# A bias load cut into five and moved behind the dense weights, to shift the final store in the round of DMA semaphores

## Chip, cores, metric

One core of one Trainium2 chip. The metric is the device time of one execution in microseconds (us). A run also has a span: the time from the first to the last instruction that the profile records on the core.

## The reference, cut to what matters

```python
def reference(A_x, A_k_cache, A_v_cache, A_wq, A_wo, B_x, B_w1, B_b1, B_w2):
    xn = _layernorm(A_x, axis=-1)                  # x: (2, 1, 448)
    # A: one decode step of attention over the last 4096 of 32768 cached rows,
    #    16 query heads on 8 key/value heads of width 256, then wo
    # B: h = xn @ w1 + b1 (1792 wide), act = h * tanh(softplus(h)), act @ w2
    return A_x + A(xn, k_cache, v_cache, wq, wo) + B(xn, w1, b1, w2)
```

The caches make up nearly all of the data: 8 heads x 2 sequences x 4096 rows x 256 x 2 bytes, for K and again for V, 67 MB of the 77.7 MB that are read.

## The kernel before

Every transfer is issued by SyncE, but for x and b1, which ScalarE issues. The framework hands each transfer one of eight DMA semaphores in turn. A transfer that gets a semaphore for the second time has to wait until the earlier one with it has landed.

```python
    x_bf = consts.tile([Bsz, D], BF16)
    nc.scalar.dma_start(out=x_bf[:, :], in_=A_x.flatten_outer_dims())
    b1_sb = consts.tile([NX, HF], BF16)                       # 2 x 896
    nc.scalar.dma_start(out=b1_sb[:, :], in_=B_b1.rearrange("(x f) -> x f", x=NX))
    ...
    for lo, hi in ((0, SC), (SC, NS)):                        # wq in two loads
        nc.sync.dma_start(out=wq_sb[:, lo:hi, :], in_=wq_in[:, lo:hi, :])
    ...
    nc.scalar.activation(out=rstd[:], in_=mv[:, 1:2], func=ACT.Sqrt, bias=eps_t[:], scale=1.0)
    ...
    def load_dense():
        ...
        nc.sync.dma_start(out=dense["w1"], in_=...)
        nc.sync.dma_start(out=dense["w2"], in_=...)

    def dense_in():
        for c in range(NF):
            for s in range(NS):
                nc.tensor.matmul(hT_ps[:, c, ...], lhsT=w1_v[:, s, c, :], rhs=xs[:, s, ...], ...)
            nc.tensor.matmul(hT_ps[:, c, ...], lhsT=b1_v[:, c, :], rhs=half[:], ...)   # adds b1
    ...
    load_k(0)
    load_dense()
    project()                    # q; ScalarE casts half of it
    build_q(0); build_q(1); turn(0)
    for i in range(Hkv + 1):     # per key/value head: load_k(i + 1), load_v(i), load_wo(i), ...
        ...
    res = consts.tile([Bsz, D], BF16)
    for n in range(NO):
        copy = nc.vector.tensor_copy if n // 2 == 0 else nc.scalar.copy
        copy(out=res[:, n * DO : (n + 1) * DO], in_=part(n))
    nc.sync.dma_start(out=out.flatten_outer_dims(), in_=res[:])      # the store
    issue_in_order(tc)           # each engine keeps the order of the text
```

The softmax here doesn't subtract the row's maximum and nothing guards it: scores larger than these inputs give would overflow.

## Time and profile before

| | before |
|---|---|
| time, median of 3 runs | 189.75 us (189.72 to 190.41) |
| profiled run: time, span | 189.68 us, 187.84 us |
| last load lands (last piece of wo) | 184.54 us |
| store issued, landed | 185.59, 186.74 us |
| store issued to end of span | 2.25 us |

The times inside a run are counted from the span's start. The SyncE timeline of the start (start, length, line, what is issued):

```profile
1.65 0.61 SPq L373 DMA_DIRECT2D k<-in_A_k_cache_dram  x1
2.30 0.58 SPq L306 DMA_DIRECT2D v<-in_B_w_dram  x1
2.93 0.44 SPq L313 DMA_DIRECT2D v<-in_B_w_dram  x1
3.41 0.55 SPq L373 DMA_DIRECT2D k<-in_A_k_cache_dram  x1
```

k0, the two dense weights and k1 are all issued within 4 us, long before they land.

### The profile page before, as it was taken

The numbers are of one execution on the slowest core, as the hardware profiler recorded it, in microseconds if no ns is written. First come the engines' busy times: TensorE is split into PE (matmuls) and PEld (weight loads), VectorE is DVE, ScalarE is ACT, GpSimd is POOL, SyncE is SP. The second block draws the span as 40 slices with busy tenths as digits, with TensorE's granted clock in tenths as the row PEclk, the third lists the DMA queues.
The fourth block names the chain that finished last, engine by engine and source line by source line (L and its number), as shares of the span: only waits on it lengthen the run. The fifth ranks groups of instructions, "written<-read, shape, count | busy, mean of one in ns | idle before, by whom it ended". The sixth has DMA issues, their size and how long they took to land.

```text
span 187.8 us, 2412 instructions
## 1 busy us (share of the span) xinstructions
PE 141.0 (75%) x938; PEld 65.0 (35%) x938; DVE 108.6 (58%) x150; ACT 45.3 (24%) x148; POOL 16.3 (9%) x74
## 2 busy tenths in 40 slices
PE   0397098904989989956896769955995779999682
PEld 0132033801334334422342324321441324444581
DVE  6703597049671994079804991099506993995201
ACT  3003115200152244024222224033302332244001
POOL 7000600300003001100030003000110000000000
PEclk9999759955899999999999999999999999999955
DMA  6999899999999999999999999999999999999990
GB/s 224 415 479 447 373 432 457 422 447 447 433 433 426 419 415 437 433 433 400 472 445 426 419 433 433 433 433 409 443 443 440 397 423 433 457 443 391 422 378 31
DMA packets 5030, 77.81 MB, mean 414 GB/s; under 512 B 534, under 2 KB 1052, under 8 KB 2332
## 3 DMA queue, kind: packets, MB, share of 16 engines
q1 hardware_dynamic: 5012, 77.66, 96.9%
q8 instruction: 7, 0.11, 0.2%
q14 instruction: 3, 0.02, 0.0%
q10 hardware_dynamic: 8, 0.01, 0.0%
HBM read 77.67 MB, written 0.00 MB: 413 GB/s over the span
## 4 chain that ended last, share of the span: by engine, by line
DMA 66%; DVE 20%; PE 8%; SPq 2%; ACT 1%; issue 1%; ACTq 0%; DVEq 0%
DMA k<-in_A_k_cache_dram 57%; DVE kt L404 16%; DMA wo<-in_A_wo_dram 9%; PE sc L416 4%; PE o L484 4%; DVE pT L442 3%; SPq L373 2%; ACT p L430 1%; PE psE L217 0%; SPq L114 0%; DVE sums L451 0%; SPq L398 0%; DVE oTm L544 0%; DVE recm L476 0%; PE psA L234 0%
## 5 line engine op out<-in xcount | busy, mean ns | idle before, releaser
L404 DVE STREAM_TRANSPOSE kt<-k 128x2048 f32<-128x2048 f32 x32 | 73.3, 2296 | 51.1 <-DMA k<-in_A_k_cache_dram 51.1
L416 PE MATMUL sc<-kt,qdiag 128*128 128x512 bf16 x256 | 62.1, 387 | 18.8 <-DVE kt L404 18.1
L430 ACT ACTIVATE p<-sc,off 128x256 bf16<-128x256 f32 x64 | 33.0, 542 | 68.4 <-PE sc L416 67.8
L484 PE MATMUL o<-v,pT 128*8 128x512 bf16 x192 | 42.5, 379 | 0.0
L416 PEld LDWEIGHTS <-qdiag 128*128 128x128 bf16 x256 | 22.9, 97 | 54.4 <-issue 16.5
L484 PEld LDWEIGHTS <-pT 128*8 128x8 bf16 x192 | 17.2, 92 | 22.4
L442 DVE STREAM_TRANSPOSE pT<-p 128x512 bf16<-128x512 bf16 x32 | 21.8, 682 | 4.7 <-ACT p L430 4.7
L286 POOL COPY qdiag<-qt 32x16 bf16<-32x16 bf16 x64 | 12.9, 247 | 120.2 <-PE sc L416 103.0
L493 ACT COPY o_sb<-o 8x512 f32<-8x512 f32 x12 | 6.3, 572 | 36.3 <-PE o L484 36.3
L430 ACT ACTIVATION_READ_ACCUMULATOR p<-sc,off 128x1 f32 x64 | 11.6, 182 | 0.0
L217 PE MATMUL psE<-wo,oTm 128*2 128x448 bf16 x24 | 5.5, 351 | 7.2 <-DVE oTm L544 7.2
L266 PE MATMUL q_ps<-v,xq 128*128 128x512 bf16 x28 | 8.7, 487 | 2.1 <-DVE xq L257 2.1
L217 PE MATMUL psE<-v,act_bf 128*2 128x448 bf16 x14 | 4.4, 493 | 7.0 <-DVE act_bf L354 7.0
L563 PE MATMUL q<-pT,v 128*128 128x4 bf16 x256 | 7.8, 169 | 2.5 <-DMA v<-in_A_v_cache_dram 2.3
L563 PEld LDWEIGHTS <-v 128*128 128x128 bf16 x256 | 7.5, 101 | 3.3 <-DMA v<-in_A_v_cache_dram 3.3
L276 DVE CAST q_sb<-q_ps 128x512 bf16<-128x512 f32 x2 | 1.3, 686 | 8.2 <-PE q_ps L266 8.2
L266 PEld LDWEIGHTS <-xq 128*128 128x128 bf16 x28 | 3.3, 121 | 7.5 <-issue 3.3
L217 PEld LDWEIGHTS <-oTm 128*2 128x2 bf16 x24 | 1.5, 82 | 11.3 <-DVE oTm L544 9.7
L217 PEld LDWEIGHTS <-act_bf 128*2 128x2 bf16 x14 | 1.4, 108 | 9.7 <-DVE act_bf L354 7.1
L190 PE MATMUL xnT_ps<-ident,xn_bf 2*128 2x2 bf16 x7 | 0.5, 166 | 5.7 <-DVE xn_bf L138 5.7
L523 PEld LDWEIGHTS q<-ident_f,o_sb 8*128 8x128 f32 x48 | 3.4, 136 | 2.5 <-issue 2.5
L276 ACT CAST q_sb<-q_ps 128x512 bf16<-128x512 f32 x2 | 1.1, 588 | 12.5 <-PE q_ps L266 12.5
(60 smaller groups left out, 49.5 us busy)
## 6 DMA issues: line engine op xcount, KB each, us to landing
k<-in_A_k_cache_dram SPq DMA_DIRECT2D x7, 4096.0 KB, 27.6
v<-in_A_v_cache_dram SPq DMA_DIRECT2D x7, 4096.0 KB, 29.6
k<-in_A_k_cache_dram SPq DMA_DIRECT2D x2, 2048.0 KB, 24.6
v<-in_B_w_dram SPq DMA_DIRECT2D x2, 1568.0 KB, 24.5
wo<-in_A_wo_dram SPq DMA_DIRECT2D x7, 448.0 KB, 30.2
v<-in_A_wq_dram SPq DMA_DIRECT2D x1, 2048.0 KB, 7.4
v<-in_A_v_cache_dram SPq DMA_DIRECT2D x1, 2048.0 KB, 15.2
v<-in_A_wq_dram SPq DMA_DIRECT2D x1, 1536.0 KB
```

The lines of the kernel that those rows point to most:

```text
L217: nc.tensor.matmul(psE[:], lhsT=lhsT, rhs=w, start=start, stop=stop, skip_group_check=True)
L266: nc.tensor.matmul(ps[u][:], lhsT=xq[:, s, :, :].rearrange("p j k -> p (j k)"), rhs=wq_sb[:, s, u * N5 : (u + 1) * N5], start=(s == 0), st ...
L286: nc.gpsimd.tensor_copy(out=tv[rows, :, e, j * Q : (j + 1) * Q : HS].rearrange("p n (b h) -> p n b h", b=Bsz), in_=qv[rows, :, h0 : h0 + r ...
L373: nc.sync.dma_start(out=t[:, cols], in_=src[:, :, cols])
L404: nc.vector.transpose(out=kt[:].bitcast(FP32), in_=k[:, half * TH * Dh : (half + 1) * TH * Dh].bitcast(FP32),)
L416: nc.tensor.matmul(psc[:], lhsT=qdiag[i % NW][:, n * NE + e, :], rhs=ktv[:, n, e, :, :], start=(n == 0 and e == 0), stop=(n == NB - 1 and ...
L430: nc.scalar.activation(out=pv[:, b, :, :], in_=sv[:, b, :, :], func=ACT.Exp, scale=scale, bias=off[:, b : b + 1], accum_out=state["rs", i] ...
L442: nc.vector.transpose(out=pT[:], in_=p_t.pop(s)[:])
L484: nc.tensor.matmul(po[:], lhsT=pT_t[i * NH + piece][:, uh * NP * Q : (uh + 1) * NP * Q : HS], rhs=v[:, u * NP : (u + 1) * NP, :].rearrange ...
L493: nc.scalar.copy(out=o_sb[:, u, :, :, :], in_=po[:, u * Dh : (u + 1) * Dh] .rearrange("r (m j) -> r j m", j=NJ) .unsqueeze(2) .to_broadcas ...
L523: nc.tensor.transpose(pqv[:, j, u, :], o_sb[:, u, j, :, :].rearrange("r h m -> r (h m)"), ident_f[0:NR, 0:NR],)
L563: nc.tensor.matmul(po[:, c, :], lhsT=vv[:, t, c, :], rhs=pTv[:, th, 0:Q:HS], start=(t == 0 and c == 0), stop=(t == T - 1), skip_group_chec ...
```

## The change

The intent: four more transfers, so that the store becomes the eighth of its round and its semaphore is the last one that the program waits for at its end. b1 was chosen to be cut up, because it is small and needed late.

```diff
     b1_sb = consts.tile([NX, HF], BF16)
-    nc.scalar.dma_start(out=b1_sb[:, :], in_=B_b1.rearrange("(x f) -> x f", x=NX))
@@ load_dense, behind w1 and w2
+        b1_in = B_b1.rearrange("(x f) -> x f", x=NX)
+        for u in range(NB1):                                  # NB1 = 5
+            cols = slice(u * HF // NB1, (u + 1) * HF // NB1)
+            nc.scalar.dma_start(out=b1_sb[:, cols], in_=b1_in[:, cols])
```

More of the change, by code (lines that the diff above doesn't have):

```diff
@@ L299 @@
     )
+    NB1 = 5
     act_bf = consts.tile([P, NF, NX, Bsz], BF16)
```

## The prediction

> **What bounds the kernel now.** I read the page first, then the DMA queue's own waits, the chain in order of time near the end, and at last the single records behind the store.
>
> ```profile
> PE 141.0 (75%) x938; PEld 65.0 (35%) x938; DVE 108.6 (58%) x150; ACT 45.3 (24%) x148; POOL 16.3 (9%) x74
> ...
> DMA  6999899999999999999999999999999999999990
> ...
> q1 hardware_dynamic: 5012, 77.66, 96.9%
> ...
> q10 hardware_dynamic: 8, 0.01, 0.0%
> ```
>
> No engine is busy throughout, but the row of the 16 DMA engines is at 8 or 9 tenths from the second slice to the last but one, and SyncE's queue alone (q1) fills 96.9% of them. ScalarE's queue (q10) holds eight packets: those of x and of the bias b1. So the body of the kernel is a full queue of loads, 77.66 MB, and only three things can move the time: the queue running dry, more work for the DMA engines, or what lies before the first byte and after the last. The chain of waits near the end (start, length, what) shows where the last byte lands:
>
> ```profile
> 163.29 0.02 issue
> 163.31 0.54 SPq L373
> ...
> 167.20 17.34 DMA wo<-in_A_wo_dram
> 184.54 0.04 issue
> 184.58 0.46 PE psA L234 x8
> 185.04 0.23 ACT res L639
> 185.28 0.27 ACTq L667
> ```
>
> The last piece of wo is issued at 167.2 and lands at 184.54, having stood 17 us in the queue. After that come the last matmuls, the four casts of the result, and the store. The span is 187.8, so 3.3 us lie behind the last load. In these the trace shows (lines of the SyncE timeline, then the instructions of the kernel's end between 186.7 and 187.15 us: durations in ns, first and last start):
>
> ```profile
> 185.59 0.33 SPq L640 DMA_DIRECT2D out_dram<-res  x1
> ```
> ```profile
> L667 SPq EVENT_SEMAPHORE  x5: 27/28/28, 186.8 to 187.0; - x5
> L667 SPq DRAIN  x2: 7/10/13, 187.1 to 187.1; - x2
> ```
>
> The store is issued at 185.59; its semaphore has its last increment at 186.743. Then SyncE runs five semaphore instructions, which start at 186.759, 186.823, 186.884, 186.949 and 187.010, and a drain at 187.075: 63 ns from one to the next, though each lasts only 28. Each of the five waits for two semaphores. By their numbers in the records: 103 and 102, 107 and 101, 108 and 100, 109 and 104, 110 and 105; the drain waits for 99. The eight DMA semaphores are 100, 101, 102, 103, 107, 108, 109, 110; 104, 105 and 99 are VectorE's, ScalarE's and GpSimd's. The store carries 103, the fourth of the eight, and it stands in the **first** of the five instructions, so the other four are walked through after it has landed.
>
> **What the Trainium skill says.** "Perfetto Trace Analysis", Identifying Dependency Chains: an instruction that has more to wait for gets EventSemaphore instructions in front of it. The trace agrees, with the five above. "Advanced Engine Details and Errata", Network/Comms: a sequencer's read of a semaphore takes 50 to 100 ns; the trace's 61 to 65 ns from one of the five to the next lie inside that. "DMA: Bandwidth & Descriptors", Why a DMA increments its semaphore by 16 and not by 1: a transfer that uses k engines has 16 - k posted at once by the sequencer and the rest as each engine's data lands. The trace agrees: b1, two partitions, has an update at 1.72 us and two single ones at 6.64 and 6.78. So each small transfer touches two DMA engines only. The same page, Specifications: below 512 B the engine does a read-modify-write. The rows of the new transfers have 358 or 360 B; no run here has such packets of data yet.
>
> **The change part by part.**
>
> 1. It removes one load of b1 from ScalarE's start (0.24 us of issue at 1.31 us). What follows there is a table load (1.58 to 2.87) and then the square root, which waits for VectorE until 4.31. The table load may begin 0.27 us earlier and then waits longer. Worth 0.
>
> 2. It adds five loads of b1 on ScalarE behind the square root. One issue costs 0.24 us (b1 before) to 0.55 us (x), so 1.2 to 2.8 us. ScalarE has nothing to do between 4.6 us and the first cast of q at 17.07 (12.5 us idle in the page's groups, waiting for PE). This is hidden, provided that none of the five waits beyond 17 us; see the rivals. The first matmul that reads b1 is at 33.77 us, and it already waits for w1 first. PE has to wait for five semaphores in place of one there, some two more semaphore instructions of 51 ns, on an engine that after these matmuls stands still for 7.0 us until VectorE has act_bf. Worth 0.
>
> 3. It moves the round. In the kernel before a load takes the semaphore of the one eight places ahead of it and waits for that one to have landed. Before: x, wq (first), b1, wq (second), k0, w1, w2, k1, then v0, wo0, k2 and so on. After: five b1 pieces stand between w2 and k1 (or about there), so k1 waits for k0, v0 for w1, wo0 for w2, and k2, v1, wo1, k3, v2 for pieces of b1. From wo2 on each waits for the same load as before, because the distance of eight doesn't change. Landings by the semaphore events: k0 21.46, w1 25.23, w2 29.00, k1 40.0 us. So k1 would be issued at 21.5 and no longer at 3.4, and it would find w1 and w2 still queued, 29.00 - 21.46 = 7.5 us of work. v0 then goes at 25.2 (before 17.5) with k1 queued, wo0 at 29.0. k2 goes at 31.5 in both, when VectorE has freed its buffer. The queue holds at least 7 us at each of these, so no byte lands later. Worth 0.
>
> 4. It moves the store. The program has 36 transfers: 9 of k, 11 of v, 9 of wo, 2 of wq, 2 dense weights, x, b1, the store. 36 = 4 x 8 + 4: the store is the fourth of its round. With four more it is number 40 = 5 x 8, the eighth. If the list at the end keeps its order, the eighth semaphore stands in the fifth of the five instructions. The four ahead wait for things long done and pass while the store is under way: it takes 186.743 - 185.917 = 0.83 us after its issue, and four of them need 4 x 63 = 0.25 us. So the end comes **0.25 us** sooner.
>
> 5. It adds packets. b1 before: on each of two DMA engines one packet of 74 ns and one of 9 ns for the semaphore, 83 ns. x, 896 B, takes 39 to 49 ns; from 74 and 44 my estimate for 358 B is 26 ns. Five of these with five times 9 ns are 175 ns, so some 0.09 us more on two of 16 engines; if the short rows cost double, 0.2 us. That counts only if one of the two is the last to finish. The last wo piece lands on its engines between 182.60 and 184.54 us, and 5 of the 16 are within 0.21 us of the last: a chance of about a half that one of the two is among these, for an expected loss of 0.03 to 0.05 us.
>
> Sum: -0.25 + 0.05 = -0.20. From 189.75 this gives **189.55 us**, 0.1% faster.
>
> **The rivals.**
>
> A. **The list at the end follows the store.** The store's semaphore is in the first instruction now; the order could be built so that the latest comes first. Then the four walks remain and the gain is 0, with the packets 189.8 us. For it: the store being first looks like more than chance. Against: the second column runs 102, 101, 100 and the first 103, 107, 108, 109, 110, which is the fixed order of the eight folded at its middle, with the store's at the fold because it is the fourth. I give the fixed order three chances in four.
>
> B. **A new wait in front runs long.** If k1 gets its place in the round ahead of the last b1 piece, that piece is the eighth after k0, and ScalarE, which issues it, stands until 21.46 us, so that its casts of q come 4.4 us late. The qt transpose, the first turn of k0 and the first scores would start some 3 us late (26.7 in place of 23.84). For it: the order of issue on two queues is not that of the program text (b1 came third in the round, not second). Against a price: VectorE waits for k1 to land at 40.03 us in any case, and k2 would be issued near 34.5 with the queue full until k1, v0 and wo0 have landed at 49 to 50. This shows in the profile and not in the time: 189.55 still.
>
> C. **The small packets hold up the big ones.** Two queues share two engines for some 10 us, and if a change between queues or short rows cost far more than the 35 ns that I took, say 0.3 us each, those two engines would be 1.5 us behind, and a full queue never gives that back: 190.5 to 191. Against: b1 and x did the same at the start, and the packets of b1 took no longer than those of 1792 B on the other queue (74 ns).
>
> D. **The lag of the DMA engines is dealt anew.** Seven instruction fetches of 16 KB, 0.88 to 0.97 us each, hit single engines, one of them at 182.27 us. The added instructions shift these by a little. It can move the end by 0.2 us either way, in no direction that I can name.
>
> **Range and chances.** The gain of 0.25 us is nearly sure in its size if the order holds; half of the doubt is D and the spread of the runs themselves (189.72 to 190.41, the profiled one 189.68), the rest A. That gives 189.15 to 190.05. A change of 2% would be 3.8 us: to be that much faster, more than the whole stretch behind the last load would have to go; to be slower, the queue would have to run dry for 3.8 us, and it has 7 in hand. So 0.01 faster, 0.98 within, 0.01 slower.
>
> **What would show it.** Right: the store's record carries the last of the eight DMA semaphores, and only one or two semaphore instructions and a drain follow its landing, the others lying before; store issue to the end of the span 2.0 us in place of 187.84 - 185.59 = 2.25; q10 with some 24 packets; k1 issued at 21.5 and its landing still near 40; the DMA row still full. Wrong: five instructions still after the landing (A); a wait of ScalarE until 21.5 us (B, harmless); packets of 358 B of over 100 ns or a last landing over 0.3 us later than 184.54 (C or D). My time would be wrong above all if the last landing moved by more than the tail gains.

## The result

| | before | after |
|---|---|---|
| time, median of 6 runs | 189.74 us (189.55 to 190.41) | 189.40 us (189.26 to 189.48) |
| mean of the same runs | 189.88 | 189.39 |
| profiled run: span | 187.84 | 187.56 |
| last load lands | 184.54 | 184.51 |
| store issued to end of span | 2.25 | 2.00 |

The ratio is 0.9974 with a 95% interval of 0.9957 to 0.9990. Ratios are the mean time of one kernel's runs over that of the other's of the same rounds, so this is not quite the ratio of the medians. The kernel is faster by 0.34 us by the medians and by 0.49 us by the means.

The page after, the rows that answer to those of before:

```profile
PE 140.9 (75%) x938; PEld 64.9 (35%) x938; DVE 108.6 (58%) x150; ACT 45.3 (24%) x148; POOL 16.3 (9%) x74
...
DMA  6999899999999999999998999999999999999991
...
q1 hardware_dynamic: 5012, 77.66, 97.0%
...
q10 hardware_dynamic: 24, 0.01, 0.0%
```

The body is as full as before, and ScalarE's queue q10 has 24 packets in place of 8. Then the chain near the end, and the store on the SyncE timeline:

```profile
167.25 17.26 DMA wo<-in_A_wo_dram
184.51 0.04 issue
184.56 0.46 PE psA L233 x7
185.02 0.23 ACT res L645
185.25 0.27 ACTq L673
```
```profile
185.56 0.33 SPq L646 DMA_DIRECT2D out_dram<-res  x1
```

The landing at 184.51 and what follows are 0.03 us earlier than before, which is nothing. The difference comes behind the store. These are the instructions of the kernel's end on SyncE between 185.9 and 186.2 us, and then between 186.7 and 187.15 us (count, durations in ns, first and last start):

```profile
L673 SPq EVENT_SEMAPHORE  x4: 28/28/28, 185.9 to 186.1; - x4
```
```profile
L673 SPq DRAIN  x3: 7/7/13, 186.8 to 187.1; - x3
L673 SPq EVENT_SEMAPHORE  x2: 17/22/28, 186.7 to 187.0; - x2
```

Four of the five waits have moved ahead of the store's landing at 186.709 us. The single records show them starting at 185.940, 186.004, 186.066 and 186.130, for semaphores 105 and 102, 106 and 101, 108 and 100, 109 and 103. The fifth, for 110 (the store's) and 104, starts at 186.726, and the drains follow at 186.791 and 186.855. (The other drain and the 17 ns semaphore instruction in the second fence belong to the barrier that ends every kernel here.) Landing to end of span took 1.097 us before and 0.846 after.

The start looks different too (SyncE timeline after):

```profile
1.65 0.62 SPq L379 DMA_DIRECT2D k<-in_A_k_cache_dram  x1
8.16 0.34 SPq L306 DMA_DIRECT2D v<-in_B_w_dram  x1
11.97 0.38 SPq L313 DMA_DIRECT2D v<-in_B_w_dram  x1
12.40 0.55 SPq L379 DMA_DIRECT2D k<-in_A_k_cache_dram  x1
```

The dense weights, not k1 alone, now wait: the first for the first piece of wq to land, the second for the second piece. k1 still lands at 40.0 us in both traces.

**What the tail does not explain.** 0.25 us is half of the 0.49 us between the means. Taking each run's span from its reported time shows the rest. After: 1.76 to 1.93 us in all six runs. For the kernel before the spans of these six runs are not listed, but every later call timed it again, and there the difference has two sizes, 1.8 to 1.9 and 2.2 to 2.4. (Spans are listed to 0.1 us, so this difference is good to 0.05.) I call the long ones **long endings**: those over 2.1 us. That is a name only: no profile was kept of such a run, so where the added time lies, before the span or behind it, is not on record.

### The profile page after: what moved, and what is told of

It is laid out like the page before. It is cut to its first block, busy times and chain, and to the rows that moved or that the text cites. A ratio compares the mean times of both kernels' runs of the same rounds, so it can differ in the third digit from the quotient of the medians.

```text
span 187.6 us, 2418 instructions
## 1 busy us (share of the span) xinstructions
PE 140.9 (75%) x938; PEld 64.9 (35%) x938; DVE 108.6 (58%) x150; ACT 45.3 (24%) x148; POOL 16.3 (9%) x74
## 4 chain that ended last, share of the span: by engine, by line
DMA 66%; DVE 20%; PE 8%; SPq 2%; ACT 1%; issue 1%; ACTq 0%; DVEq 0%
DMA k<-in_A_k_cache_dram 57%; DVE kt L410 16%; DMA wo<-in_A_wo_dram 9%; PE sc L422 4%; PE o L490 4%; DVE pT L448 3%; SPq L379 2%; ACT p L436 1%; PE psE L216 0%; SPq L113 0%; DVE sums L457 0%; SPq L404 0%; DVE oTm L550 0%; DVE recm L482 0%; PE psA L233 0%
## 5 line engine op out<-in xcount | busy, mean ns | idle before, releaser
L490 PEld LDWEIGHTS <-pT 128*8 128x8 bf16 x192 | 17.2, 92 | 22.4
L216 PE MATMUL psE<-v,act_bf 128*2 128x448 bf16 x14 | 4.9, 533 | 7.0 <-DVE act_bf L360 7.0
L265 PE MATMUL q_ps<-v,xq 128*128 128x512 bf16 x28 | 7.5, 435 | 2.1 <-DVE xq L256 2.1
L529 PE MATMUL q<-ident_f,o_sb 8*128 8x8 f32 x48 | 3.9, 204 | 0.0
```

The source lines that it names most:

```text
L216: nc.tensor.matmul(psE[:], lhsT=lhsT, rhs=w, start=start, stop=stop, skip_group_check=True)
L265: nc.tensor.matmul(ps[u][:], lhsT=xq[:, s, :, :].rearrange("p j k -> p (j k)"), rhs=wq_sb[:, s, u * N5 : (u + 1) * N5], start=(s == 0), st ...
L490: nc.tensor.matmul(po[:], lhsT=pT_t[i * NH + piece][:, uh * NP * Q : (uh + 1) * NP * Q : HS], rhs=v[:, u * NP : (u + 1) * NP, :].rearrange ...
L529: nc.tensor.transpose(pqv[:, j, u, :], o_sb[:, u, j, :, :].rearrange("r h m -> r (h m)"), ident_f[0:NR, 0:NR],)
```

## The experiments

Theory T: the gain is the tail alone, set by the store's place in the round. Rival S: the later loads or b1's new place bring it. Theory E, formed after after_again: of the gain a part lies outside the span, and it depends on the number of ScalarE's instructions. "Tail" is from the store's issue to the end of the span, in the profiled run. All kernels gave correct results.

| run | transfers, store's place | more ScalarE instructions | tail us | long endings | mean us | before, same call |
|---|---|---|---|---|---|---|
| before | 36, 4th | 0 | 2.25 | 17 of 42 | | |
| after (first call) | 40, 8th | 4 | 2.00 | 0 of 6 | 189.39 | 189.88 |
| after_again | 40, 8th | 4 | 1.99 | 0 of 6 | 189.38 | 189.99 |
| behind_one | 36, 4th | 0 | 2.23 | 3 of 6 | 190.05 | 189.99 |
| front_five | 40, 8th | 4 | 1.99 | 0 of 6 | 189.45 | 189.99 |
| wq_six | 40, 8th | 0 | 1.99 | 2 of 6 | 189.72 | 189.99 |
| behind_three | 38, 6th | 2 | 2.13 | 0 of 6 | 189.65 | 189.75 |
| behind_six | 41, 1st | 5 | 2.10 | 0 of 5 | 189.58 | 189.75 |
| behind_thirteen | 48, 8th | 12 | 1.99 | 0 of 5 | 189.39 | 189.75 |
| scalar_pad | 36, 4th | 4 | 2.24 | 0 of 6 | 189.75 | 189.75 |
| scalar_pad_again | 36, 4th | 4 | 2.25 | 0 of 6 | 189.68 | 189.78 |
| vector_pad | 36, 4th | 0 | 2.24 | 2 of 6 | 189.85 | 189.78 |
| wq_six_pad | 40, 8th | 4 | 1.98 | 0 of 5 | 189.57 | 189.78 |
| scalar_pad_one | 36, 4th | 1 | 2.24 | 1 of 5 | 189.81 | 189.78 |

The kernel before was timed 11, 11, 11 and 9 times, with 7, 4, 2 and 4 long endings.

### The store's place apart from b1's place

**after_again**, the changed kernel once more.

> The changed kernel once more, beside the three others of this call. Theory T (the gain is the tail: the store's semaphore is in the last of the five closing waits): 0.25 us under the kernel before, store issue to end of span 2.00 us against 2.25. Rival S (the gain is in the loads: w1, w2 and k1 are issued later, and the DMA engines end more evenly, so that the slow runs of 190.2 to 190.4 us go away): 0.3 to 0.5 us under it, with no run above 189.6, while before has again some above 190.

Measured: 189.38 against 189.99 us, ratio 0.9968 (0.9948 to 0.9989). The spans average 187.53 against 187.85, the time outside 1.84 against 2.13. So 0.32 us of the gain are inside, of which the tail is 0.26, and 0.29 outside.

**behind_one**: b1 behind the dense weights, but whole.

```diff
-    NB1 = 5
+    NB1 = 1
```

> b1 in one load behind the dense weights, so 36 transfers and the store fourth in its round as before. T: the time of before within 0.1 us, five semaphore instructions after the store has landed, tail 2.25 us. S, or a gain from b1 leaving the front: 0.2 us or more under before although the tail is 2.25.

Measured: ratio 1.0004 (0.9983 to 1.0024), tail 2.23 us, all five semaphore instructions after the store's landing, three long endings of six:

```profile
L673 SPq EVENT_SEMAPHORE  x5: 28/28/28, 187.0 to 187.2; - x5
```

Moving b1 gains nothing that shows. By the time alone a gain of up to 0.3 us would lie within the interval; the next run, which has the gain with b1 in front, settles it.

**front_five**: b1 in five pieces at its old place.

```diff
-    nc.scalar.dma_start(out=b1_sb[:, :], in_=B_b1.rearrange("(x f) -> x f", x=NX))
+    for u in range(NB1):                                      # NB1 = 5
+        cols = slice(u * HF // NB1, (u + 1) * HF // NB1)
+        nc.scalar.dma_start(out=b1_sb[:, cols], in_=b1_in[:, cols])
```

> b1 in five loads at its old place in the front, so 40 transfers, the store eighth. T: tail 2.00 us, 0.25 us under before, unless the four added issues on ScalarE (1.1 us at 0.27 each) delay the square root and q: the table load would end at 4.0 in place of 2.9, before 4.3, so no. S: nothing gained beyond what the early waits of w1 and w2 do; if those are the cause, they may appear here too, and the tail decides.

Measured: ratio 0.9972 (0.9954 to 0.9991), tail 1.99, no long ending. The gain comes without moving b1: 0.54 us of the mean, where after_again had 0.61. In its trace the dense weights are issued at 8.38 and 8.76 us, so the later loads came along; the next run has the tail with less of that.

**wq_six**: b1 untouched, wq in six loads.

```diff
-    for lo, hi in ((0, SC), (SC, NS)):
+    for lo, hi in ((0, 1), (1, 2), (2, 3), (3, SC), (SC, SC + 1), (SC + 1, NS)):
```

> b1 untouched; wq in six loads and not two, so again 40 transfers and the store eighth, with no transfer under 512 B added. T: 0.25 us under before, tail 2.00 us, as the changed kernel. If the short rows of b1 cost time on two DMA engines (my step 5, at most 0.2 us), this is that much faster than the changed kernel; four more issues of 0.4 us on SyncE delay k0 and the dense weights by 1.6 us in the queue's order, which has 3.5 MB of wq to move meanwhile, so 0.

Measured: tail 1.99 us, dense weights at 4.46 and 5.11 us, ratio 0.9987 (0.9966 to 1.0007). Four of the five closing waits stand ahead of the store's landing at 186.86 us, as in the changed kernel:

```profile
L667 SPq EVENT_SEMAPHORE  x4: 28/28/28, 186.1 to 186.3; - x4
```

So the tail gains its 0.25 us with four more transfers of either kind, of b1 or of wq, and without a late issue of the dense weights. But two of six runs have long endings, and the last load of the profiled run lands at 184.66, 0.1 us later than before. So it falls short of the changed kernel by 0.34 us: two long endings of some 0.4 us in six make 0.13 of that, and the rest is in the span (187.75 in the mean against 187.53). Packets below 512 B can't be its cause, since this kernel has none of data added. The traces point to another: wq now comes in packets of 4096 and 8192 B in place of 16384 and 12288, and all wq packets together take 9.5 us on each DMA engine in the mean, where the kernels with wq in two loads have 9.2 to 9.4. Some 0.2 to 0.3 us more work in a queue that is never empty would be of the size of what is missing; that is an estimate, and a landing at 184.66 still lies among those of the other traces (184.41 to 184.93).

### The closing waits as a folded list

**behind_three** and **behind_six**: NB1 = 3 and NB1 = 6.

> b1 in three loads behind the dense weights: 38 transfers, the store sixth. Theory T (the closing waits go through a fixed list folded at its middle, so a store at place 4, 5, 6, 7 or 8 stands in the first to fifth of five): the store's semaphore in the third of five, two passed before its landing, two after it, store issue to end 2.25 - 0.125 = 2.12 us. Rival E (of what the change gained, a part lies outside the span: the reported time less the span is 1.8 us in some runs and 2.3 in others; 8 of 17 runs of before, 0 of 18 runs of the kernels with four more instructions on ScalarE): with two more instructions on ScalarE it is open whether the long case comes; it tells where the change of state lies.

> b1 in six loads: 41 transfers, the store first in its round. T, folded list: the first of the eight stands in the third instruction, as the sixth does, so the tail is 2.12 us and 0.13 longer than with five. If the list were simply ordered with the first in front, all of five would follow: 2.25. E: five more instructions on ScalarE, no run with 2.3 us outside the span.

The kernel's end on SyncE behind the store, first behind_three, then behind_six:

```profile
L673 SPq EVENT_SEMAPHORE  x5: 28/28/28, 185.9 to 186.8; - x5
```
```profile
L673 SPq EVENT_SEMAPHORE  x5: 28/28/691, 185.8 to 186.7; - x5
```

In behind_three two of the five start before the store has landed (185.877 and 185.941) and the third, with the store's 108, at 186.667 just after it. In behind_six, whose store is first in a new round, the third instruction waits for 108 and for the store's 100; it starts early and lasts 691 ns in place of 28. The tails are 2.13 and 2.10 us, where 2.12 was expected. So place 1 and place 6 share the third instruction, and the fold holds at the four places tried (1, 4, 6 and 8): the first column of the five is the fourth to eighth semaphore of the round, the second column the third, second and first, then VectorE and ScalarE. The eighth place is the best of the four; by the list it is the best of all eight. The times agree in order, but at 5 or 6 runs the ratios, 0.9995 and 0.9990, both have intervals across 1.

### The price of the small packets, and ScalarE held up

**behind_thirteen**: NB1 = 13.

> b1 in thirteen loads of 136 to 138 B a row: 48 transfers, the store eighth again. T: tail 2.00 us as with five. It triples the suspected cost of the small packets (26 packets of data on two DMA engines, and the same of semaphores): by my step 5 with the 22 ns that the changed kernel's trace shows for 358 B, eight more transfers cost 8 x (22 + 9) = 0.25 us at most on each of the two, and 0 to 0.25 at the end; rival C (switching between queues is dear) says 1 us or more. E: none of its runs with 2.3 outside.

Measured: ratio 0.9980 (0.9967 to 0.9993), tail 1.99, last load landed at 184.42, the same as with five (184.51) within 0.1. With 26 packets of b1, each 13 or 14 ns by the trace, no loss shows at the end. It also brought about what rival B of the prediction described, since late pieces of b1 wait here for k0. Its ScalarE timeline, with the casts of q; its PE timeline at the first scores; the waits of ScalarE up to 40 us; and its DMA row:

```profile
4.32 18.05 ACTq L321 DMA_DIRECT2D b_sb<-in_B_b_dram  x13
22.41 1.07 ACT L275 CAST q_sb<-q_ps 128x512 bf16<-128x512 f32 x2 [17.80 <-DMA b_sb<-in_B_b_dram]
```
```profile
27.01 8.27 PE L422 MATMUL sc<-kt,qdiag 128*128 128x512 bf16 x25 [10.47 <-DVE kt L410]
```
```profile
ACT q_sb L275 <- DMA b_sb<-in_B_b_dram: 17.8, 1, 17.8
```
```profile
DMA  6999899999999999999999999999999999999991
```

ScalarE hangs in its own issues until 22.4 us and the first scores start at 27.0 and not at 23.8, yet the DMA row stays full and the end doesn't move. Three microseconds lost at the start of the compute cost nothing that shows.

### What lies outside the span

**scalar_pad**: before, with four useless copies on ScalarE.

```diff
+    pad = consts.tile([Bsz, 4], FP32)
+    for u in range(4):
+        nc.scalar.copy(out=pad[:, u : u + 1], in_=eps_t[:])
     nc.vector.reciprocal(out=rstd[:], in_=rstd[:])
```

> The kernel before with four useless copies of two elements on ScalarE behind the square root, results unused; 36 transfers, store fourth, nothing else changed. T alone: the time of before, tail 2.25, and the same mix of runs with 1.8 and 2.3 us outside the span. E (the number of instructions on ScalarE decides it, whatever they are): span as before, 187.8, but all runs at 1.8 outside, so a median 0.2 to 0.4 us under that of before and none over 190.

Measured: 1.79 to 1.89 us outside the span in all six runs, where before in the same call had 4 long ones of 11. But the mean is 189.75 as before's, since its spans were longer this time (187.90 against 187.77 in the mean; the profiled one 188.2 with the last load at 184.93). The expected gain of 0.2 to 0.4 in the median did not come.

**scalar_pad_again**, for the count.

> The kernel before with four useless copies on ScalarE, once more, for the count: E says no run with over 2.1 us outside the span (0 of 6 the first time; before has 12 of 28 so far), T says tail 2.25. Its spans of 187.7 to 188.2 the first time should lie with those of before in this call, 187.7 to 188.2.

Measured: 1.75 to 1.92 us outside in all six runs, spans of 187.8 to 188.0 as before's, mean 189.68 against 189.78. (The count of 12 of 28 in the expectation is 11 of 22 and one of the first result's runs, whose spans are not listed: it takes the one at 190.41 for a long ending and leaves out the one at 190.18, which may be either.)

**vector_pad**: the same four copies on VectorE.

> The kernel before with the four useless copies on VectorE in place of ScalarE; store fourth. T: tail 2.25, span as before. E says that ScalarE's instructions count and not any four more: some runs, two or three of six, have 2.2 us or more outside the span as before has. If none has, the state is not tied to ScalarE and my reading of the padded kernel falls.

Measured: two long endings of six (2.17 and 2.23). So not any four instructions remove them; of the two engines tried it is ScalarE's that count.

**wq_six_pad**: wq_six and scalar_pad together.

> wq in six loads (40 transfers, the store eighth) and four useless copies on ScalarE; b1 in one load at its old place. If the gain of the changed kernel is just T (0.25 us in the closing waits) and E (no run with 2.2 to 2.4 us outside the span), this has both: tail 2.00 us, all runs below 2.1 outside, 0.3 to 0.6 us under before by the mean, without the change itself. If b1's move had a part of its own, it stays above the changed kernel's 189.3 to 189.4.

Measured: tail 1.98, 1.80 to 1.82 us outside in all five runs, mean 189.57 against 189.78, ratio 0.9988 (0.9976 to 1.0000). Both parts are there without touching b1, as T and E say. But the gain of the mean, 0.21, is less than the 0.3 to 0.6 expected, and the time stays above the changed kernel's 189.3 to 189.4, which the expectation would have read as a part of its own for b1's move. front_five speaks against that reading: it has 189.45 with b1 in front. The span average is 187.76, only 0.09 under before, although the tail is 0.28 shorter; the last load landed at 184.70 in its trace. So what the tail gains is in part missing from the span in both kernels with wq in six loads; the longer packet time given under wq_six, 9.5 us here too, is of that size.

**scalar_pad_one**: one useless copy.

> The kernel before with one useless copy on ScalarE, store fourth. In the traces so far an instruction fetch of 8192 B on the queue q14 starts 1.0 us after the span's end where ScalarE has four or five instructions more, 1.7 us after it with two more, inside the span with twelve more, and is in no trace with none more. If that fetch is ScalarE's and its place decides about the long runs, one more instruction puts it later than 1.7 us after the end or out of the record, and the time outside the span should be at or above that with two more (1.85 to 2.05 us), with some runs above 2.1. If the number of ScalarE instructions only has to differ from that of before, all runs are at 1.75 to 1.95. Tail 2.25 and span as before in either case.

Measured: 1.86 to 2.11 us outside, as the first of the two readings said, but with only one run of five above 2.1, and that one by 0.01 (by the span of its trace it is 2.09). The records of the queue q14, whose packets the page calls "instruction", give this order:

| more ScalarE instructions | start of the fourth 8192 B fetch on q14 since the span's start, from the span's end | time outside the span |
|---|---|---|
| 0 (before, behind_one, wq_six, vector_pad) | none in any of the four traces | 1.8 to 1.9 or 2.2 to 2.4 us |
| 1 | 2.02 us after | 1.86 to 2.11 |
| 2 | 1.70 us after | 1.85 to 2.05 |
| 4 or 5 (seven traces) | 1.00 to 1.01 us after | 1.75 to 1.99 |
| 12 | 13.6 us before | 1.75 to 1.86 |

Over all kernels, those with two or more additional ScalarE instructions have 0 long endings in 51 runs, those with none 24 in 60. The count of the long endings is firm. The fetch moves earlier as ScalarE's program gets longer, in one trace or a few for each length, and the long endings are gone when it is recorded at 1.70 us or sooner. That the program's end sometimes stands waiting for this fetch is the plain reading, but it is not shown.

One record comes near it. Behind the span the traces hold one update each of the semaphores 7 to 255, in five runs of numbers. The run 54 to 104 starts 0.82 or 0.83 us after the span's end in eleven traces (0.90 in behind_six, where all five are later), but 1.23 in behind_three and 1.11 in scalar_pad_one, the two with the fetch at 1.70 and 2.02. So something is held up by 0.3 to 0.4 us there. Yet the last semaphore update on record comes no later in these two than in the changed kernel (1.90 and 1.91 against 1.91 us), so this delay is not seen to reach the end. What the long endings wait for stays open.

## Why the prediction was right, and where it was not

- **What bounds the kernel:** right. The DMA row is as full in every run's profile, and the one large delay of the compute (behind_thirteen) cost nothing.
- **Part 1, b1 leaves the front, worth 0:** right (behind_one, 1.0004).
- **Part 2, five issues hidden on ScalarE:** right. They took 4.32 to 5.8 us, at 0.24 to 0.29 each, and the first matmul with b1 started at 33.8 us in both. The added instructions on ScalarE, which I called worth 0, went with a gain by another way: see the last point.
- **Part 3, the round:** wrong in its order, right in its price, and that in part by luck. I put the five pieces between w2 and k1. The semaphore numbers after show them as the fourth, fifth, sixth, eighth and ninth transfer, with k0 the seventh, so that the dense weights waited for wq and went at 8.16 and 11.97 us, and k1 at 12.4 and not 21.5. The round goes through the transfers of both queues, and the program's text fixes the order on each queue alone; that b1 came third before, and not second, could have warned me. The price was 0 for a reason that I had not given: the dense weights were issued while k0, which landed at 21.50 us, was still under way, and w1 landed at 25.22 us (25.23 before).
- **Part 4, the store eighth, 0.25 us:** right. 0.258 us between the two tails, and the places 1, 4, 6 and 8 are as the folded list says.
- **Part 5, small packets, 0.05 us:** if anything too high. The 358 B packets took 22 ns (estimate 26), and eight more transfers than five cost nothing to be seen.
- **Rival A** (the list follows the store) fell with the first trace. **Rival B** did not occur in the changed kernel, but did in behind_thirteen, with the first scores at 27.0 us (26.7 in the text) and no cost. **Rival C** fell there as well. **Rival D**, the lag of the DMA engines dealt anew, stays open: the spans spread from 187.7 to 188.2 for one and the same kernel, but nothing ties that to the fetches of 16 KB.
- **What I had left out:** I took the 1.8 us outside the span for a constant, and the runs of 190.4 for spread. Part of them are runs with some 0.4 us more outside the span, 17 of 42 of before and none of 12 of the changed kernel. In the call of after_again this is 0.29 of the 0.61 us by which the mean gained; for the 0.49 of the first call the spans of before are not listed. So the sum, -0.20, lacked a term, and 189.55 was 0.15 above the median measured. The range had room for it: that it held is owed in part to its width, not only to the sum. The added copies of scalar_pad and scalar_pad_again removed the long endings and yet gained little by the mean (0.00 and 0.10 us), so this term by itself is shown in the time outside the span and not clear of noise in the whole time.

The changed kernel had the largest gains over before in these calls. behind_thirteen has the same mean (189.39), on another chip, so nothing was found that is surely better.

## What to carry to other kernels

When the DMA engines are full from start to end, look behind the last load: the order in which the closing waits stand can be read off the semaphore numbers in the trace, and a store that stands in the last of them lets the others pass while it is under way. Take the span from each run's time before explaining a gain of a few tenths: part of it may lie where the span does not reach, and there the number of instructions on one engine, useless or not, went with 0.4 us in some of the runs. And to price a suspected wait or small transfer, multiply it: thirteen pieces told more than five.

## What the Trainium skill lacked or had wrong

- No page that I read tells of the closing waits of a program: five semaphore instructions in a fixed folded order, 61 to 69 ns from one to the next, so that the store's place in the round of eight is worth up to 0.25 us. "Advanced Engine Details and Errata", Network/Comms, gives 50 to 100 ns for reading a semaphore; these steps lie inside that, though no run shows that they are such reads.
- "Runtime: NRT & Kernel Launch", Instruction fetch mechanics, has instructions fetched in blocks of 16 KiB and calls the cost of crossing a boundary mostly hidden. The traces have seven fetches of 16384 B inside the span, and three of 8192 B besides, with a fourth that moves with the length of ScalarE's program. In the kernels whose traces show it at 1.70 us after the span's end or sooner, none of 51 runs had the 0.4 us more outside the span; where no trace shows it, 24 of 60 had. Whether the fetch is the cause is open.
- "DMA: Bandwidth & Descriptors", Specifications, has transfers below 512 B done as read-modify-write. These runs don't show it wrong: packets of 136 to 360 B took 13 to 22 ns each, fewer bytes in a ns than those of 896 B (39 ns and up), and whether a read-modify-write was among it no run tells. What they add is that 26 such packets on a second queue cost nothing at the end that shows.
